# RetNet attention feeding a SwiGLU block: the last 64 tokens of the first batch entry are taken out of the opening and done later, some of q arrives in longer runs, and twelve products are halved

## The chip, the cores and the metric

The kernel runs on one core of a Trainium2 chip. The metric is the device time of one execution in microseconds (us). The engines named below are PE (TensorE: matrix products, with its weight loads listed as PEld), DVE (VectorE), ACT (ScalarE), POOL (GpSimd) and SP (SyncE, which here only issues DMAs). ACT issues DMAs as well.

## The reference

The inputs q, k, v have the shape (8, 8, 576, 64): batch, heads, tokens, head width. The weights are 512 x 1536 (gate and value) and 1536 x 512 (out), all 8 bytes per number in memory.

```python
scores = scale * np.matmul(q, k.transpose(0, 1, 3, 2))
gamma = 1.0 - 2.0 ** (-5.0 - np.arange(H, dtype=np.float32))
Dmat = np.where(rel >= 0, gamma[:, None, None] ** rel[None, :, :], 0.0)   # rel = token i - token j
attn_out = np.matmul(scores * Dmat[None], v)                              # (B, H, S, D)
x = np.ascontiguousarray(attn_out.transpose(0, 2, 1, 3)).reshape(B * S, H * D)   # 4608 x 512
g = x @ w_gate
silu = g * (1.0 / (1.0 + np.exp(-g)))
out = silu * (x @ w_val) @ w_out
```

Because of the causal decay, attention can be done in chunks of 64 tokens: each chunk needs its own 64 x 64 score block and one 64 x 64 state that sums up all chunks before it. 576 tokens are nine chunks, and 576 = 4 x 128 + 64.

## The kernel before, in words

**Attention** works on pairs of heads. There are 8 batch entries of 4 pairs, so pairs 0 to 31; `HP` is 4. `load(i)` (L271) issues the DMAs of pair i. `tick(t)` (L678) is one step of a pipeline three pairs deep: it brings pair t into the right layout (`transposes`), computes scores and states of pair t-1 (`scores`, `new_states`, and the DVE work in `masked`), and finishes pair t-2 (`own_values`, `earlier_values`, then `to_x`, which scales the result by the decay of each row and writes it into x, the transposed input of the second block).

**The first batch entry** (pairs 0 to 3, ticks 0 to 5 with `hi == HP`) is done in an opening in which nothing else can run. There, q and k are transposed by PE through PSUM banks (L471) and copied out by DVE or ACT (L472). The ninth chunk has its own small transposes (L476) and copies (L479), its own scores (L566), mask (L589), values (L554) and a last output (L651). q arrives unscaled, and `to_x` multiplies on DVE (L627, L640).

**The second block** takes x in tiles of columns. The first tile has 512 tokens (`up0`, L767, then `down0`); its weights arrive as 8-byte numbers and are turned into 4-byte ones by two ACT passes (`split`, L404 and L405) and two DVE instructions (`rounding`, L418 and L419). `up0(f, chunks)` multiplies weight block f of gate and value with x, 512 columns at a time. Two `up0` blocks start in the opening. The rest, f = 2 to 11, stand in a list called `plan` (from L1109), with the ticks of the second batch entry between them: tick 4 after f = 2, tick 5 after f = 3, tick 6 after f = 5. From L1163 on, tiles of 1024 tokens use a fast multiplication scheme written out in tables (`up_step` L1003, `down_step` L1050), with the remaining ticks among them.

**What sets the order.** L1085 fixes the order of every engine's instructions, SP's too, to that of the program text: each engine works through its list in order, and an instruction that waits holds up all that follow on the same engine. DMAs issued by SP and by ACT share eight completion semaphores, handed out in turn, so that a DMA waits for the landing of the eighth DMA before it in the order in which the program was laid out, whichever of the two engines issued that one. The list of SP around the change is: the loads of pairs 0 to 3 and small tables, eight weight pieces and more (L385), `load(4)` (`load(HP)`, L1091, emitted in tick 3), one gate weight block (L385), `load(5)` (`load(HP + 1)`, L1097), then `load(6)` (from `next_load`, L1122). ACT issues the later weight loads between its passes (L385 for up weights, L387 for w_out).

The index i of `load(i)`, the argument of `up0` and the argument of `tick` are used below as in the code.

Of the kernel before, what the change touches and what calls it, by code (L numbers as in the profile page):

```python
# [22 lines left out]
def tables(gamma, scale, L):  # L23
# [12 lines left out]
    pieces = scale * np.stack(half, axis=2).reshape(2 * L, -1)  # L36
    parts = [twice((g[:, None] ** -at).T), twice((g[:, None] ** (L - at)).T),
             both(g[:, None] ** L), both(g[:, None] ** (2 * L)), pieces, both(scale * g[:, None] ** at),
# [116 lines left out]
def kernel(  # L155
# [32 lines left out]
    nc = tc.nc  # L188
# [65 lines left out]
    io = const.tile([P, 1024], F32, name="io")  # L254

# [8 lines left out]
    def whole(i):  # L264

        return i < needed(2) - 2
# [4 lines left out]
    def load(i):  # L271
# [6 lines left out]
        if i < HP:  # L278
            qk = late[0] if late else ld.tile([P, 2, S // SQ, SQ], F32, tag="qk", name="qk").rearrange("p n j d -> p (n j d)")[:, 0 : NC * D]
            queues = (nc.sync, nc.scalar if i < 2 else nc.sync)  # L280
            for dst, src in ((qk, q), (kn, k)):
                dst = dst.rearrange("p (g d) -> p g d", d=D)
                for n, at in enumerate((slice(0, NFULL + 1), slice(NFULL + 1, NC))):
                    queues[n].dma_start(out=dst[:, n::2], in_=tokens(src, b, p)[:, at])
            queues[i % 2].dma_start(out=t.rearrange("p (g d) -> p g d", d=D), in_=tokens(v, b, p))
# [21 lines left out]
    def chunk(i, hl, c, paired=False):  # L307

        if whole(i):
            g, r = divmod(NC * hl + c, 2)  # L310
            g = 2 * g % NC if paired else g
            return half[r], slice(g * D, (g + 1) * D)
        if c + 1 == NC:
            return half[hl], slice(CW, CW + D)
        return half[c % 2], slice((2 * (c // 2) + hl) * D, (2 * (c // 2) + hl + 1) * D)

    def column(i, hl, c):

        return ts((c - hl) % NC if i < HP else c, L)
# [6 lines left out]
    NCOL = 2 * H + 4 * HP  # L326
# [8 lines left out]
    piece = tab[:, NCOL - 2 * HP : NCOL]  # L335
# [12 lines left out]
    decay(slice(0, H), slice(0, H), half[0])  # L348
    decay(odd_heads, even_heads, half[1])
    decay(even_heads, odd_heads, half[1])  # L350
    nc.gpsimd.tensor_copy(out=last_near, in_=near[:, even_heads])
# [71 lines left out]
    for f in range(2):  # L423
        for m in range(2):
# [8 lines left out]
    spare = rest[:, dn_at + 2560 : sum_at]  # L433
    other = (spare[:, 0:CW].rearrange("p (h c i) -> p h c i", h=2, i=L), spare[:, CW : CW + L],
             spare[:, 640 : 640 + NC * D].rearrange("p (c d) -> p c d", d=D))
    early = [spare[:, 640 + S * (1 + i) : 640 + S * (2 + i)] for i in range(HP)]
# [6 lines left out]
    def last_scores(i):  # L443
        return bankE[:, 0:L] if i < HP else sr
# [14 lines left out]
    def transposes(i):  # L459
# [7 lines left out]
        if i < HP:  # L467

            for t, src, bank in ((kT, kn, bankB), (qT, qk, bankA)) if i else ((qT, qk, bankA), (kT, kn, bankB)):
                for c in range(NFULL):  # L470
                    nc.tensor.transpose(bank[:, ts(c, P)], src[:, ts(c, P)], ident)  # L471
                copy(t[:, 0:CW], bank)  # L472
            tails = ((kT, kn), (qT, qk))
            for n, (_, src) in enumerate(tails):
                for hl in range(2):
                    nc.tensor.matmul(bankC[half[hl], ts(n, L)], src[half[hl], CW : CW + D], ident[half[hl], half[hl]],  # L476
                                     start=True, stop=True, skip_group_check=True)
            for n, (t, _) in enumerate(tails):
                copy(t[:, CW:S], bankC[:, ts(n, L)])  # L479
# [13 lines left out]
        def keys():  # L493
            blocks = kn.rearrange("p (g d) -> p g d", d=D)
            if i < HP:
                parts = [(0, every, blocks[:, 0 : NC - 1 : 2]), (1, every, blocks[:, 1:NC:2]), (1, half[1], blocks[half[1], NC - 1])]
            elif whole(i):
# [38 lines left out]
    def new_states(i):  # L536
        s = st[i]
        for c in range(NFULL):
            for r in range(2):
                for hl in range(2):  # L540
                    rows, at = chunk(i, hl, 2 * c + r)
                    nc.tensor.matmul(z[half[hl], r, c], s["kn"][chunk(i, hl, 2 * c + r, i < HP)], s["v"][rows, at],  # L542
                                     start=True, stop=True, skip_group_check=True)

    def earlier_values(i):
# [6 lines left out]
        for hl in range(2):  # L552
# [3 lines left out]
        for c in (1, 3, 4, 6, 5, 7, 2, 8) if whole(i) else range(1, NC):  # L556
            for hl in range(2):
                nc.tensor.matmul(xr[half[hl]] if c + 1 == NC else value(i, hl, c), state[half[hl], c, :],  # L558
                                 s["qT"][half[hl], column(i, hl, c)], start=False, stop=True, skip_group_check=True)
# [656 lines left out]
```

## Time and profile before

| | |
|---|---|
| time, three runs | 1041.9 us median, 1040.08 to 1045.64 |
| the profiled execution: its own time / its span | 1040.84 us / 1039.1 us |
| PE busy | 1025.6 us, 99% of the span |
| PE busy before 26.39 us, when `up0` begins | 18.91 of 26.39 us |
| PE busy from 44.00 to 73.00 us | 29.0 of 29.0 us |
| DVE, ACT, POOL busy | 642.3, 297.4, 400.5 us |
| mean busy share of the 16 DMA engines, first 26.39 us | 1.00 |
| the same, 44.00 to 52.30 / 52.30 to 59.60 us | 0.95 / 0.84 |
| PE clock granted | 0.999 |

Lines such as L772 are those of the kernel before. In a row of the timeline the first number is the start (us from the start of the span), the second the time to the end of the last instruction of the row, then follow engine, line, operation, what is written and read, how many, and in brackets the time that the engine idled before and what ended it. One product of 4-byte numbers is two matmul records[...]. SPq and ACTq rows are DMA issues, not transfers.

### The profile page before, as it was taken

Reading aid. Unit: us, or ns where it says so; the run is one execution under the profiler, and the core shown is the slowest. Engines: PE = TensorE matmul, PEld = TensorE weight load, DVE = VectorE, ACT = ScalarE, POOL = GpSimd, SP = SyncE. Lnnn points to the kernel's source line nnn. Section 1 sums busy time; section 2 is a strip of 40 time slices with the busy share of each in tenths; the row PEclk is TensorE's granted clock in tenths of the full one; section 3 lists DMA queues with packets and bytes.
Section 4 is the critical chain, followed back from the end, with each engine's and each line's share of the span. In section 5 each row is a group of like instructions: output and inputs, shape, how many; then the busy total and the mean of one; then the engine's idle time right before and its main releaser. Section 6 shows DMA issues by size and latency. Waiting matters only on the chain.

```text
span 1039.1 us, 21528 instructions
## 1 busy us (share of the span) xinstructions
PE 1025.6 (99%) x8448; PEld 843.2 (81%) x8448; DVE 642.3 (62%) x1091; ACT 297.4 (29%) x646; POOL 400.5 (39%) x347
## 2 busy tenths in 40 slices
PE   7999999999999999999999999999999999999998
PEld 6444555888888888888888888888888888888887
DVE  5588868776768767546458785435466644344644
ACT  4475433243544222222322103223211022231110
POOL 2002376766565036522133058212240583222505
PEclk9999999999999999999999999999999999999999
DMA  9999877776679887674676686545554465555653
GB/s 244 251 283 276 190 208 270 195 212 191 195 190 256 213 249 217 186 196 134 186 229 173 176 202 216 152 138 153 158 172 150 143 195 154 152 153 162 180 162 100
DMA packets 310380, 199.10 MB, mean 192 GB/s; under 512 B 220168, under 2 KB 254984, under 8 KB 310280
## 3 DMA queue, kind: packets, MB, share of 16 engines
q1 hardware_dynamic: 279000, 161.51, 57.3%
q10 hardware_dynamic: 31280, 36.22, 10.4%
q8 instruction: 67, 1.10, 0.4%
q14 instruction: 33, 0.27, 0.1%
HBM read 157.56 MB, written 40.11 MB: 190 GB/s over the span
## 4 chain that ended last, share of the span: by engine, by line
PE 78%; DVE 2%; issue 1%; ACT 0%; DVEq 0%
PE bankC L1003 13%; PE bankE L1003 13%; PE bankB L1003 13%; PE bankA L1003 13%; PE bankB L1050 6%; PE bankC L1050 6%; PE bankA L1050 6%; PE bankE L1050 6%; PE outer L531 1%; PE inner L572 1%; PE outer L558 1%; PE inner L542 1%; DVE rest L806 1%; DVE arena L806 0%; DVE rest L940 0%
## 5 line engine op out<-in xcount | busy, mean ns | idle before, releaser
L940 POOL TENSOR_TENSOR rest<-rest 128x512 f32<-128x512 f32 x65 | 91.6, 1414 | 299.1 <-DVE rest L940 279.8
L1024 ACT ACTIVATE io<-rest 128x256 f32<-128x256 f32 x180 | 74.8, 416 | 303.5 <-DVE rest L940 260.8
L1003 PE MATMUL bankC<-rest,arena 128*128 128x256 f32 x544 | 129.1, 380 | 0.0
L1003 PE MATMUL bankA<-rest,arena 128*128 128x256 f32 x544 | 128.7, 379 | 0.0
L806 POOL TENSOR_TENSOR arena<-arena 128x512 f32<-128x512 f32 (+1 forms) x72 | 111.5, 1561 | 36.1 <-DMA up<-arena 23.9
L1003 PE MATMUL bankE<-rest,arena 128*128 128x256 f32 x512 | 121.4, 380 | 0.9 <-DVE rest L940 0.9
L1003 PE MATMUL bankB<-rest,arena 128*128 128x256 f32 x512 | 121.2, 379 | 0.0
L1031 POOL TENSOR_TENSOR arena<-rest,io 128x256 f32<-128x256 f32 x72 | 51.9, 726 | 167.8 <-ACT io L1024 167.8
L1003 PEld LDWEIGHTS bankA<-rest,arena 128*128 128x128 f32 x544 | 103.2, 190 | 14.5 <-issue 0.5
L1003 PEld LDWEIGHTS bankC<-rest,arena 128*128 128x128 f32 x544 | 102.9, 190 | 14.6 <-POOL arena L806 0.3
L1003 PEld LDWEIGHTS bankE<-rest,arena 128*128 128x128 f32 x512 | 96.9, 190 | 14.6 <-DVE rest L940 1.4
L1003 PEld LDWEIGHTS bankB<-rest,arena 128*128 128x128 f32 x512 | 97.1, 190 | 13.3
L806 POOL TENSOR_TENSOR rest<-rest 128x256 f32<-128x256 f32 (+1 forms) x66 | 67.4, 1042 | 95.9 <-DMA qk<-in_k_dram 60.1
L940 DVE TENSOR_TENSOR rest<-bankB,rest 128x512 f32<-128x512 f32 x72 | 48.9, 687 | 67.4 <-PE bankB L1003 51.5
L940 DVE TENSOR_TENSOR rest<-bankC,rest 128x512 f32<-128x512 f32 x72 | 48.9, 687 | 65.8 <-PE bankC L1003 47.1
L940 DVE TENSOR_TENSOR rest<-bankA,rest 128x512 f32<-128x512 f32 x72 | 48.9, 687 | 61.5 <-PE bankA L1003 44.1
L940 DVE TENSOR_TENSOR rest<-bankE,rest 128x512 f32<-128x512 f32 x71 | 48.2, 687 | 60.0 <-PE bankE L1003 46.7
L1027 DVE SCALAR_TENSOR_TENSOR arena<-rest,io 128x256 f32<-128x256 f32 x84 | 58.5, 698 | 11.1 <-ACT io L1024 11.0
L1050 PE MATMUL bankB<-arena 128*128 128x256 f32 x252 | 58.3, 381 | 0.3 <-DVE arena L806 0.3
L1050 PE MATMUL bankA<-arena 128*128 128x256 f32 x252 | 58.0, 380 | 0.2 <-DVE arena L806 0.2
L1050 PE MATMUL bankC<-arena 128*128 128x256 f32 x252 | 58.1, 380 | 0.0
L1050 PE MATMUL bankE<-arena 128*128 128x256 f32 x252 | 57.9, 379 | 0.0
(192 smaller groups left out, 1617.0 us busy)
## 6 DMA issues: line engine op xcount, KB each, us to landing
arena<-up SPq DMA_DIRECT2D x234, 256.0 KB, 2.6
arena<-dn SPq DMA_DIRECT2D x104, 384.0 KB, 3.8
up<-arena ACTq DMA_DIRECT2D x78, 256.0 KB, 4.1
dn<-rest SPq DMA_DIRECT2D x78, 128.0 KB, 1.9
out_dram<-rest SPq DMA_DIRECT2D x31, 256.0 KB, 4.1
qk<-in_q_dram SPq DMA_DIRECT2D x108, 72.0 KB, 2.3
qk<-in_k_dram SPq DMA_DIRECT2D x108, 72.0 KB, 3.3
rest<-in_moe_w_out_dram ACTq DMA_DIRECT2D x6, 1024.0 KB, 5.1
```

The lines of the kernel that those rows point to most:

```text
L531: m = nc.tensor.matmul(value(i, hl, c), s["v"][rows, at], ret[rows, c % 2 if whole(i) else hl, c // 2], start=start, stop=start, skip_grou ...
L542: nc.tensor.matmul(z[half[hl], r, c], s["kn"][chunk(i, hl, 2 * c + r, i < HP)], s["v"][rows, at], start=True, stop=True, skip_group_check= ...
L558: nc.tensor.matmul(xr[half[hl]] if c + 1 == NC else value(i, hl, c), state[half[hl], c, :], s["qT"][half[hl], column(i, hl, c)], start=Fal ...
L572: nc.tensor.matmul(sc[chunk(i, hl, 2 * c + r)[0], r if whole(i) else hl, c], kT[half[hl], at], qT[half[hl], at], start=True, stop=True, sk ...
L806: eng.tensor_tensor(out=dst, in0=srcs[0], in1=srcs[1], op=ALU.add if op[0] == "add" else ALU.subtract)
L940: eng.tensor_tensor(out=at(op[1]), in0=at(op[2]), in1=at(op[3]), op=ALU.add if op[0] == "add" else ALU.subtract)
L1003: m = nc.tensor.matmul(b[:, gv * TB : (gv + 1) * TB], w[:, gv, ts(c, P)], rhs[:, c, :], start=(opens and gv == 0 and c == 0), stop=(c == 1 ...
L1024: nc.scalar.activation(out=s, in_=src[:, 0:TB], func=AF.Silu, scale=-1.0 if negative else 1.0)
L1027: return lambda: nc.vector.scalar_tensor_tensor(out=dst, in0=src[:, TB : 2 * TB], scalar=-1.0, in1=s, op0=ALU.mult, op1=ALU.mult)
L1031: nc.gpsimd.tensor_tensor(out=dst, in0=src[:, TB : 2 * TB], in1=s, op=ALU.mult)
L1050: nc.tensor.matmul(b[:, m * TB : (m + 1) * TB], lhs[:, qd, ts(m, P)], w[:, qd], start=(opens and qd == 0 and m == 0), stop=(qd == NQ - 1), ...
```

## The change

- **Ninth chunk.** In the opening, pairs 0 to 3 are loaded, transposed and multiplied only for tokens 0 to 511 (`CW`). The work of L476, L479, L554, L566, L589 and L651 is gone from there. The last state of each pair is written to a new place, `end_states`.
- **Where it goes.** `end_loads` issues 20 DMAs on SP after `load(5)`: 16 that bring q and k of the 64 tokens of all eight heads, 16 KB each in runs of 128 bytes, and four for v. `end_transposes` (two DVE block transposes of 128 x 256) stands in `plan` ahead of tick 5; `end_scores` (8 products) follows the scores of pair 4 on PE inside tick 5; `end_masks` (two DVE multiplies) closes the DVE pieces of tick 5; `end_own`, `end_earlier` (8 products each) and `end_to_x` (three DVE multiplies) are in tick 6.
- **q of pairs 1 to 3** is loaded with four consecutive tokens per partition, in runs of 1 KB rather than 256 bytes, into `early[i]`; `scale_run` multiplies it on POOL by the scale and the row's decay while regrouping it, and `transposes` undoes the interleaving while copying out of PSUM. `to_x` of these pairs is then a plain copy on ACT instead of a multiply on DVE.
- **Loads of pairs 0 to 3** go by head: six DMAs of 128 KB per pair instead of five of 288, 160 or 128 KB.
- **Order in tick 3.** `split(0)` moves ahead of pair 1's values, and the transposes of pair 3 move behind `to_x` of pair 1.
- **Decay tables.** The opening builds them with two POOL instructions instead of three; the swapped halves and `last_near` are made after `load(5)`. The table of `run` adds 32 columns to the first small DMA.
- **Twelve products.** `up0(2)` (gate and value) and the gate half of `up0(3)` do each of their four products as two of 256 columns.

```diff
-        return i < needed(2) - 2
+        return HP <= i < needed(2) - 2
+
+    def scaled(i):
+
+        return 0 < i < HP
...
-            for dst, src in ((qk, q), (kn, k)):
-                dst = dst.rearrange("p (g d) -> p g d", d=D)
-                for n, at in enumerate((slice(0, NFULL + 1), slice(NFULL + 1, NC))):
-                    queues[n].dma_start(out=dst[:, n::2], in_=tokens(src, b, p)[:, at])
-            queues[i % 2].dma_start(out=t.rearrange("p (g d) -> p g d", d=D), in_=tokens(v, b, p))
+            for h, queue in zip(heads, queues):
+                if scaled(i):
+                    queue.dma_start(out=early[i][:, ts(h % 2, CW // 2)], in_=q[b, h, 0:CW].rearrange("(p c) d -> p (c d)", c=NFULL))
+                else:
+                    queue.dma_start(out=blocks(qk)[:, h % 2], in_=q[b, h, 0:CW].rearrange("(c p) d -> p c d", p=P))
+            for h, queue in zip(heads, queues):
+                queue.dma_start(out=blocks(kn)[:, h % 2], in_=k[b, h, 0:CW].rearrange("(c p) d -> p c d", p=P))
+            for h in heads:
+                queues[i % 2].dma_start(out=blocks(t)[:, h % 2], in_=v[b, h, 0:CW].rearrange("(c p) d -> p c d", p=P))
...
+                if scaled(i):
+                    nc.scalar.copy(out=dst(lo, end)[to].rearrange("p (c r i) -> p c r i", r=2, i=L)[:, :, r], in_=xo[src, :, r])
...
+    def end_loads():
+        for n, src in enumerate((q, k)):
+            for a in range(P // SQ):
+                for j in range(2):
+                    nc.sync.dma_start(
+                        out=end_raw[a * SQ : (a + 1) * SQ, n].rearrange("t (n j d) -> t n j d", n=HP, d=SQ)[:, :, j],
+                        in_=src[0, a // 2 : H : 2, CW + j * SQ : CW + (j + 1) * SQ, (a % 2) * SQ : (a % 2 + 1) * SQ].rearrange("n t d -> t n d"))
+        for hl in range(2):
+            for x in range(2):
+                nc.sync.dma_start(out=end_v[half[hl ^ x], 2 * x : 2 * x + 2],
+                                  in_=v[0, 4 * x + hl : 4 * x + 4 : 2, CW:S].rearrange("n t d -> t n d"))
+    def end_transposes():
+        for n, to in enumerate((end_q, end_k)):
+            nc.vector.transpose(out=to.rearrange("p n i -> p (n i)"), in_=end_raw[:, n])
+    def end_scores():
+        for n, x, hl in ends:
+            nc.tensor.matmul(end_at[x][half[hl ^ x], n], end_k[half[hl], 2 * x + n], end_q[half[hl], 2 * x + n],
+                             start=True, stop=True, skip_group_check=True)
+    def scale_run(i):
+        if scaled(i):
...
+            nc.gpsimd.tensor_tensor(out=dst, in0=src, in1=table, op=ALU.mult)
...
+            scale_run(t + 1)
             if lo < t < hi:
                 new_pair()
+            if t + 1 == HP:
+                split(0)
             if lo <= t - 2 < hi:
                 own_values(t - 2)
-            for f in transposes(t) if lo <= t < hi else ():
+            for f in transposes(t) if lo <= t < hi and t + 1 < HP else ():
                 f()
-            if t + 1 == HP:
-                split(0)
...
+            for f in transposes(t) if t + 1 == HP else ():
+                f()
...
             scores(t - 1, t - 2 < lo)
+            if t == HP + 1:
+                end_scores()
...
+                if f == 2 or f == 3 and gv == 0:
+                    for m in range(2):
+                        nc.tensor.matmul(bank[:, ts(m, TB)], w, xs[0][:, c, ts(m, TB)],
+                                         start=(c == 0 and m == 0), stop=(c == HP - 1), skip_group_check=True)
+                    continue
...
     load(HP + 1)
+    for to, heads in ((even_heads, odd_heads), (odd_heads, even_heads)):
+        decay(heads, to, half[1])
+    nc.gpsimd.tensor_copy(out=last_near, in_=near[:, even_heads])
+    end_loads()
...
+            if tick_at[f] == HP + 1:
+                plan.append(end_transposes)
             plan.append(lambda t=tick_at[f]: tick(t, HP, FIRST))
```

## The prediction

> **What bounds the kernel now.** I read the page first. PE is busy almost throughout; the only slice below nine tenths is the first.
>
> ```profile
> PE 1025.6 (99%) x8448; PEld 843.2 (81%) x8448; DVE 642.3 (62%) x1091; ACT 297.4 (29%) x646; POOL 400.5 (39%) x347
> ...
> PE   7999999999999999999999999999999999999998
> ```
>
> So a change pays only by shortening the opening, and whatever stops PE later is lost in full: no engine can catch up for it. The timeline of PE shows where the opening ends and what stops it last: the values of pair 2 wait for `to_x` of pair 1 on DVE, and `up0` starts at 26.39.
>
> ```profile
> 24.88 1.01 PE L531 MATMUL outer<-ret,v 64*64 64x64 f32 x32 [1.52 <-DVE rest L627]
> ...
> 26.39 0.70 PE L772 MATMUL bankA<-rest,arena 128*128 128x512 f32 x1
> ```
>
> Next, the place where the moved work goes, tick 5. PE computes pair 4's states (L542) and scores (L566, L572) at 57.8 and goes straight on with `up0(4)` at 59.01; these rows show no idle time:
>
> ```profile
> 57.81 0.69 PE L542 MATMUL inner<-v,kn 64*64 64x64 f32 x32
> ...
> 58.44 0.64 PE L572 MATMUL inner<-qT,kT 64*64 64x64 f32 x30
> 59.01 3.70 PE L772 MATMUL bankA<-rest,arena 128*128 128x512 f32 x8
> ```
>
> Last, SP's timeline and its waits, because the moved chunk must first be loaded and its 20 DMAs stand behind `load(5)`:
>
> ```profile
> 49.01 2.77 SPq L293 DMA_DIRECT2D qk<-in_k_dram  x4
> 51.87 0.45 SPq L298 DMA_DIRECT2D kn<-in_k_dram  x1
> 59.57 0.39 SPq L298 DMA_DIRECT2D v<-in_v_dram  x1
> 60.05 4.10 SPq L293 DMA_DIRECT2D qk<-in_q_dram  x4
> ```
>
> ```profile
> SPq L298 <- DMA rest<-in_moe_w_out_dram: 9.0, 2, 7.2
> ```
>
> v of pair 5 is issued at 59.57, 7.2 us after the DMA ahead of it. It waits for a w_out block that ACT issued at 53.16: that DMA is the eighth before it, and the two share a completion semaphore. SP passes the end of `load(5)` at 59.96, after PE has gone through the place where `end_scores` will stand.
>
> ACT's timeline says why w_out is late: its `split` waits 5.71 us for the gate block that SP issued at 43.10.
>
> ```profile
> 50.74 0.67 ACT L404 ACTIVATE rest<-rest 128x512 f32<-128x512 f32 x1 [5.71 <-DMA rest<-in_moe_w_gate_dram]
> ...
> 53.16 0.39 ACTq L387 DMA_DIRECT2D rest<-in_moe_w_out_dram  x1
> ...
> 57.36 0.37 ACTq L385 DMA_DIRECT2D rest<-in_moe_w_val_dram  x1
> ```
>
> **What the Trainium skill says.** "DMA: Bandwidth & Descriptors", section "Anatomy of one DMA — SWDGE (gpsimd) path", says that DMA engines never wait on semaphores; the issuing sequencer waits before it dispatches. The trace agrees: for those 7.2 us SP issues nothing. The same section puts a DMA's fixed cost at about 2 us; here four k pieces landed a median 2.2 us after issue (48 to 52 us) and 5.3 us under a weight load (64 to 68 us). "Why small descriptors are slow (HBM only)" on that page charges a fixed overhead per packet; from 5 to 13 us, all in 256-byte runs, the trace has 281 GB/s, against 369 to 430 in slices where 2 KB runs dominate. "TensorE: Matmul & The Clock Gate", section "Architectural detail", lets PE pull only weight loads ahead of running products; the trace of before cannot show whether `up0(4)` could overtake a waiting `end_scores`, and I take it that it cannot.
>
> **The change, part by part.**
>
> *The opening.* Per pair the tails (L476, two small copies L479) go: in tick 3 they take PE from 21.72 to 22.27, and elsewhere the scores start about 0.4 us after the big q copy could have allowed them (tick 1: that copy ends at 12.60, scores start at 13.03). Over ticks 0 to 2 about 1.0 us stays on the path. The reordering of tick 3 lets PE do pair 3's transposes (1.1 us) after pair 1's values, beside `to_x`, and takes most of the 1.52 us wait away; `to_x` moves to ACT (three copies, 0.37 each by `even`'s L583), behind `split(0)` (two passes, 0.67 each). Estimate: `up0` starts 2.6 us earlier, between 1.5 and 3.5.
>
> *DMA.* 4 pairs x 3 tensors x 128 runs = 1536 runs of 256 bytes go (0.39 MB; at 281 GB/s 1.4 us). q of three pairs, 0.79 MB, in 1 KB runs at perhaps 370 instead of 281 GB/s saves 0.7. Together SP and the weights come 2.1 us earlier. `scale_run` has not been traced; POOL's 128x512 multiply (L940) takes 1.41 us, three of them 4.2 us on an engine busy 7.29 us of the first 26.39. It stands ahead of the keys of pairs 2 and 3 on POOL, so a late q would delay those by at most its lateness. I take zero; 1 us at worst, spent in the opening.
>
> *Twelve products.* 48 half-width records in place of 24. Full ones come every 0.43 us; halves in the later tiles (L1003) every 0.215 (eight in 1.72 us), with a weight load of 190 ns under each. Cost 0; at worst 48 x 0.025 = 1.2 us.
>
> *The moved work.* 24 products = 48 records on PE. The 32 records of L558 take 0.57 us there (73.95 to 74.52), so 0.9 us. DVE gains two transposes (128x576 takes 0.77, so 0.35 each), two masks and three scalings, about 2 us in all, which lie under `up0`.
>
> *The wait.* `end_scores` needs both `end_transposes`, and these need the 16th DMA of `end_loads`. Before time minus 2.1: w_out lands at 57.4 (59.5 before), v of pair 5 goes then, E1 to E3 to 59.2. E4 stands where the DMA eight before it is the next weight block (issued by ACT at 57.36 before; SP got past it at 62.58), so 60.4. Twelve more issues at about 0.45 us (rows of 0.39 to 0.50 where SP is free): E16 at 65.8. Landing 2.2 to 5.3, I take 3: 68.8. DVE: +0.7 = 69.5. In before's time PE left this point at 59.01. **Delay 10.5 us, plus 0.9 for the moved products: 11.4.** The opening's 2.6 us do not count: PE only reaches the wait earlier (about 56.4) and stands there for some 13 us. Behind `end_scores` on PE are `up0(4)` and everything after; behind `end_transposes` on DVE the masks of pair 4 and the roundings, which hold up `split` on ACT. After the release, DVE stands to PE about as before (60.30 against 59.01), so I add nothing for it; `load(6)` follows the 20 issues and keeps its distance to tick 6.
>
> Sum on the profiled execution: 1040.84 + 11.4 = 1052.2. This execution lies 1.1 us below the median. The positions of the shared semaphores are the least known term and the errors I can name (0.35 us per issue, a quick landing) shorten the wait, so I put the likeliest at 1051.
>
> **Rivals.**
>
> *A. SP is not held behind w_out.* If the layout gives other eighth neighbours, v goes at 49.8 + 0.5, 16 issues take 7.2, landing 2.2, transposes 0.7: release at 60.4, 1.4 us after 59.01; with 0.9, +2.3 us: 1043 (1041 to 1046). For: the number of DMAs ahead changes. Against: all move by the same four places, and w_out and the value block are still among the eight in front of some E; whichever waits for w_out cannot go before 57.
>
> *B. The loads arrive before PE needs them* (the other side). Then the opening's 2.6 us stay, less 0.9: 1039. It decides at a landing of E16 by 55.7 (PE at 56.4, less 0.7), so E1 would have to be issued by 55.7 - 2.2 - 15 x 0.45 = 46.7; SP is at the last of `load(5)`'s k at 49.8 even unhindered. PE would show no gap at tick 5.
>
> *C. A longer hold.* The gate block that ACT issued at 61.93 (landing at about 67.5 before, when ACT's L404 at 67.87 waits for its queue) is the eighth before one of E9 to E16, and the stalled DVE makes later weights late too: another 3 to 6 us, 1055 to 1058. For: its issue lies just after those of `load(5)`.
>
> **How the numbers follow.** Main case 0.66 (1047 to 1055); A 0.18; B 0.07; C 0.07; something in the opening worth over 5 us 0.02. About 0.5% (5 us) is what a measurement of this kernel tells from no change. Slower takes the main case, C and a sliver of A: 0.75; same is A and B: 0.23; faster 0.02, since even B gives only 0.2%. The range 1042 to 1056 leaves out B, most of C and the edges; the main case's own is 1047 to 1055.
>
> **What would show it.** Right: one idle stretch of PE of 8 to 15 us ahead of the first `end_scores` product, released by DVE's transpose, itself released by a DMA into `rest` from q or k; `up0` at about 24; no idle time at the halved products; SP's 20 issues starting only after a wait for a weight DMA. Wrong: the issues start before 50 us, PE passes tick 5 without a gap, or products behind `end_scores` run ahead of it.

## The result, and the profile after

The changed kernel takes 1058.3 us (median of four runs, 1056.81 to 1058.58) beside 1041.5 us for the kernel before (1040.08 to 1045.64). The ratio is 1.0147, with an interval of 1.0125 to 1.017: 15 us slower by the ratio, 17 by the two medians. The forecast of 1051.0 had the direction, but the time lies above its range (1042 to 1056).

One execution of each kernel was profiled; that of the changed one took 1058.58 us with a span of 1056.9. Its page (busy time by engine, then tenths of 40 slices and the granted TensorE clock in the same slices):

```profile
PE 1024.3 (97%) x8440; PEld 845.0 (80%) x8440; DVE 640.9 (61%) x1078; ACT 300.2 (28%) x648; POOL 401.6 (38%) x349
...
PE   6949999999999999999999999999999999999998
...
PEclk9979999999999999999999999999999999999999
```

PE's busy time is 1.3 us less than before, while the span is 17.8 us longer: PE does not work more, it stands. The third slice (53 to 79 us) shows it with a 4, and a clock of seven tenths. A record below is one matmul instruction as the profile lists it. PE's timeline there (start, duration, engine, line, operation; in brackets the idle time ahead and what ended it):

```profile
57.09 0.67 PE L574 MATMUL inner<-qT,kT 64*64 64x64 f32 x30
72.44 0.71 PE L704 MATMUL outer<-rest 64*64 64x64 f32 x16 [14.67 <-DVE rest L698]
73.07 4.99 PE L852 MATMUL bankA<-rest,arena 128*128 128x512 f32 x8
```

PE finishes the scores of pair 4 at 57.76 and then waits 14.67 us for the second DVE transpose of the moved chunk. `up0(4)` starts at 73.07 instead of 59.01, 14.06 us later. Its first eight records take 4.99 us; before they took 3.70.

SP's timeline and its waits from 40 to 75 us show where the transposes' data was:

```profile
39.15 4.50 SPq L392 DMA_DIRECT2D rest<-in_moe_w_gate_dram  x1
...
59.54 0.38 SPq L311 DMA_DIRECT2D v<-in_v_dram  x1
60.02 5.24 SPq L688 DMA_DIRECT2D rest<-in_q_dram  x8
65.37 5.01 SPq L688 DMA_DIRECT2D rest<-in_k_dram  x8
```

```profile
SPq L311 <- DMA rest<-in_moe_w_out_dram: 7.4, 1, 7.4
SPq L392 <- ACT rest L412: 4.0, 1, 4.0
SPq L688 <- DMA rest<-in_moe_w_val_dram: 1.5, 1, 1.5
SPq L688 <- DMA rest<-in_q_dram: 1.1, 1, 1.1
```

v of pair 5 is issued at 59.54, no earlier than before (59.57), after the same wait for w_out. The fourth of the 20 loads waits for the value block, and the eleventh waits 1.1 us for the fourth. (The trace also holds the number of each DMA's completion semaphore: w_out and v have 102, the value block, the fourth and the eleventh load 106.) The line with 4.0 us is taken up below, where the prediction is compared. The sixteenth load, the last one of k, goes at 69.95, and on DVE the transposes follow their loads:

```profile
68.45 0.45 DVE L698 STREAM_TRANSPOSE rest<-rest 128x256 f32<-128x256 f32 x1 [8.59 <-DMA rest<-in_k_dram]
71.93 0.45 DVE L698 STREAM_TRANSPOSE rest<-rest 128x256 f32<-128x256 f32 x1 [3.04 <-DMA rest<-in_k_dram]
```

The rest of the trace adds little. `up0` starts at 23.63 instead of 26.39, and in this execution the loads gain nothing from it: v and w_out come when they came before. (Traces of one opening differ: three with that of before start `up0` at 25.12, 26.39 and 27.61, the fourteen with the new one between 23.63 and 25.46. The means lie 1.9 us apart.) In tick 6 the moved products add 0.78 us. In the second tile PE waits twice more, where the kernel before has one wait of 0.95 us at 190.80:

```profile
204.24 1.96 PE L1082 MATMUL bankA<-rest,arena 128*128 128x256 f32 x8 [1.68 <-DVE rest L1019]
...
210.43 1.99 PE L1082 MATMUL bankC<-rest,arena 128*128 128x256 f32 x8 [0.51 <-POOL arena L1053]
```

PE starts the second tile 16.17 us later than before (190.32 against 174.15), and from the 201st record of that tile on it is 17.7 us late, to the end. The following comparison of starts (us, one profiled execution each) serves all the experiments:

| kernel | first down product | second tile | its 201st record | last product |
|---|---|---|---|---|
| before | 123.77 | 174.15 | 218.88 | 1034.91 |
| after | 139.94 | 190.32 | 236.62 | 1052.67 |
| chunk not moved | 121.62 | 175.66 | 223.18 | 1038.84 |
| scores one tick later | 125.97 | 177.87 | 223.53 | 1040.29 |
| loads first | 128.87 | 181.22 | 228.22 | 1045.06 |
| v of pair 5 behind the loads | 139.91 | 190.29 | 234.06 | 1050.28 |
| loads on GpSimd's queue | 130.26 | 180.64 | 225.21 | 1041.97 |
| the same, transposes ahead of `up0(3)`'s product | 128.93 | 179.78 | 225.25 | 1043.25 |
| the same, ahead of `up0(2)`'s product | 124.13 | 176.47 | 222.00 | 1038.78 |
| before, 13.8 us of products | 137.00 | 187.50 | 230.96 | 1047.58 |
| after, stretch filled | 137.31 | 188.93 | 234.13 | 1049.82 |
| after, products undivided | 144.65 | 196.29 | 240.58 | 1056.36 |
| before, v of pair 5 cut in five | 124.65 | 175.03 | 219.10 | 1035.35 |

### The profile page after: what moved, and what is told of

Same layout as the page of the kernel before. It is cut to its first block, busy times and chain, and to the rows that moved or that the text cites. A ratio compares the mean times of both kernels' runs of the same rounds, so it can differ in the third digit from the quotient of the medians.

```text
span 1056.9 us, 21545 instructions
## 1 busy us (share of the span) xinstructions
PE 1024.3 (97%) x8440; PEld 845.0 (80%) x8440; DVE 640.9 (61%) x1078; ACT 300.2 (28%) x648; POOL 401.6 (38%) x349
## 3 DMA queue, kind: packets, MB, share of 16 engines
q10 hardware_dynamic: 30784, 36.18, 10.3%
## 4 chain that ended last, share of the span: by engine, by line
PE 67%; DVE 3%; SPq 1%; ACT 1%; issue 0%; DMA 0%; ACTq 0%; POOL 0%; DVEq 0%
PE bankE L1082 11%; PE bankC L1082 11%; PE bankB L1082 10%; PE bankA L1082 10%; PE bankB L1129 6%; PE bankA L1129 5%; PE bankC L1129 5%; PE bankE L1129 5%; PE outer L533 1%; PE outer L560 1%; PE inner L574 1%; PE inner L544 1%; SPq L306 1%; DVE rest L885 1%; DVE rest L1019 0%; DVE arena L1106 0%
## 5 line engine op out<-in xcount | busy, mean ns | idle before, releaser
L1019 DVE TENSOR_TENSOR rest<-bankC,rest 128x512 f32<-128x512 f32 x72 | 48.9, 688 | 65.8 <-PE bankC L1082 47.1
L1019 DVE TENSOR_TENSOR rest<-bankE,rest 128x512 f32<-128x512 f32 x71 | 48.3, 688 | 59.5 <-PE bankE L1082 46.6
```

The lines of the kernel that those rows point to most:

```text
L1019: eng.tensor_tensor(out=at(op[1]), in0=at(op[2]), in1=at(op[3]), op=ALU.add if op[0] == "add" else ALU.subtract)
```

## The experiments

**Is it SP's order and the shared semaphores?** Four kernels change where the loads stand, or when they are needed.

Leave the moved chunk out (the last 64 tokens of the first batch entry are missing from the output; their columns of x are set to zero):

```diff
-    end_loads()
+    nc.gpsimd.memset(xs[1][:, :, 0:L], 0.0)
```

and without the calls of `end_transposes`, `end_scores`, `end_masks`, `end_own`, `end_earlier`, `end_to_x`.

> The changed kernel without the moved chunk: its 20 loads, transposes, scores, masks, values and scalings are left out, so the 64 tokens of the first batch entry are missing from the output (their columns of x are zero). Theory (the loss is PE's wait for the moved loads): no idle stretch at tick 5, up0 at about 23.6 us, a time of 1041.5 less 2.8 for the opening and less up to 1 us at the second tile, 1037.5 to 1039.5 us. Rival (the opening's other edits, q through POOL, the loads by head or the halved products, cost time further on): over 1045 us.

Measured 1045.71 us, ratio 1.0031 (1.0015 to 1.0047). The stretch in tick 5 is gone: `up0(4)` starts at 56.86. But the time is not 1039: it lies where the rival had it, over 1045. The first down product is 2.15 us earlier than before, and the last product is 3.9 us later. What takes it back is treated below.

Need the scores one tick later:

```diff
-            if t == HP + 1:
+            if t == HP + 2:
                 end_scores()
```

with `end_transposes` and `end_masks` in that tick as well, and `end_own`, `end_earlier`, `end_to_x` in the next.

> The loads stay where they are; the transposes, scores and masks of the moved chunk go from tick 5 to tick 6, its values and scalings from tick 6 to tick 7. Theory: the last k load lands at about 72 us, PE reaches tick 6 at about 71 us, so at most 1 us of idle time is left there and the time is 1039 to 1042 us. Rival (20 small DMAs on SP cost as much wherever the products stand, since the loads of pairs 6 and 7 come 13 us later behind them): PE waits at tick 6 or 7 for these pairs instead, 1048 us or more.

Measured 1050.04 us, ratio 1.0083 (1.0056 to 1.0111). The stretch shrinks from 14.67 to 1.96 us, at 74.53, so the wait is one for data that comes at a fixed time. The whole time was missed and lies where the rival had it, though the wait that is left in tick 6 is for the transposes of the moved chunk, not for pairs 6 and 7: the profiled run, the quickest of its four (1046.2), already shows 1.29 us of waiting at 166.84.

Put the 20 loads ahead of those of pair 5:

```diff
+    end_loads()
     load(HP + 1)
     ...
-    end_loads()
```

> The 20 loads stand ahead of the load of pair 5 instead of behind it. In this layout the w_out block is the eighth DMA before the 16th load. Theory (position in SP's queue and the shared semaphore make the wait): the first 15 go between 44 and 52 us, the 16th when w_out has landed, 57 to 60 us; PE idles at tick 5 until 60 to 62 us, for 2 to 5 us; the time is 1042 to 1047 us. If only the number of DMAs mattered: the idle stretch stays near 14 us and moves to pair 5, 1055 us or more. If neither the semaphore nor w_out mattered: no idle stretch, 1039 to 1041 us.

Measured 1049.99 us, ratio 1.0072 (1.0053 to 1.0092); PE waits 3.62 us at 61.13. Same loads, same bytes, eleven microseconds less of a wait. The sixteenth load went at 57.27, when w_out had landed, as expected. The whole time was again missed, by later waits (1.44 us at 147.45, 2.36 at 195.83).

Put v of pair 5 behind the 20 loads, so that the first of them, not v, is the eighth DMA behind w_out:

```diff
-            for dst, src in ((kn, k), (t, v)):
+            for dst, src in ((kn, k), (t, v))[: 1 if i == HP + 1 else 2]:
```

and v of pair 5 after `end_loads()`.

> The v load of pair 5 stands behind the 20 loads instead of ahead of them; now the first of the 20 is the eighth DMA behind w_out. Theory (whatever stands eighth is held): the first load is issued at 59 to 60 us, as the v load was, and PE idles 13 to 15 us at tick 5. Rival (the v load waited for its own buffer): the first load is issued at about 52 us and the idle stretch shrinks to 7 or 8 us.

Measured 1056.2 us, in one execution. SP's timeline, then PE's:

```profile
50.92 0.44 SPq L311 DMA_DIRECT2D kn<-in_k_dram  x1
59.59 4.38 SPq L688 DMA_DIRECT2D rest<-in_q_dram  x8
```

```profile
71.43 0.71 PE L704 MATMUL outer<-rest 64*64 64x64 f32 x16 [14.39 <-DVE rest L698]
```

Now a load of q stands for w_out, up to the same 59.6 us. What waits is the place, whichever transfer holds it (here w_out and this load of q have semaphore 102). With the run before this, that shows the prediction's mechanism.

**The loads on another queue.** GpSimd's queue instead of SyncE's:

```diff
-                    nc.sync.dma_start(
+                    nc.gpsimd.dma_start(
                         out=end_raw...
```

(and the same for `end_v`).

> The 20 loads of the moved chunk go through GpSimd's queue instead of SyncE's; nothing else differs from after. Theory (the 14.7 us stretch comes from SyncE's issues standing behind w_out and the gate block through shared semaphores): the loads no longer stand there, they are issued from about 40 us on, and the idle stretch of PE at end_scores falls from 14.7 to between 0 and 5 us. For the whole time the theory says no more than what the run with the scores one tick later showed: 1044 to 1050, since the later passages take some back. Rival (the 20 loads are slow in themselves, by their small runs): the stretch stays above 10 us and the time at 1055 to 1060.

Measured 1047.09 us, ratio 1.005 (1.0035 to 1.0065), beside 1058.3 (1.0147) for the change as it is, and as expected. The 20 loads are issued from 31.88 to 46.7 us and have all landed at 51.83, so small runs were not the trouble. PE still waits 2.83 us at 61.24, for a transpose that DVE did at 60.43, behind its product of `up0(3)`.

Move the transposes ahead of that product too:

```diff
+        if f == 3:
+            plan.append(end_transposes)
         plan.append(lambda f=f: up0(f, range(HP)))
...
-            if tick_at[f] == HP + 1:
-                plan.append(end_transposes)
```

> The 20 loads on GpSimd's queue as in the earlier run, and the two DVE transposes ahead of the product of up0(3) instead of behind it. Theory (what was left there, 2.83 us, was DVE's order, not the loads): PE passes tick 5 with no idle time over 0.3 us, at about 58 us. Time: down0 then starts at about 127.5, some 3.5 us behind before; with the passage up to 200 us taking 0 to 3 us, 1044 to 1048. Rival (POOL's issues or the loads themselves cost it): the idle time stays above 2 us.

Measured 1046.01 us, ratio 1.0037 (1.0022 to 1.0052). Its time was met, its reason was not: 2.08 us of waiting are left, as the rival had it. DVE's timeline shows that the rival's cause is not it either: the data has long landed, but the roundings of the weights (L425, L426) stand ahead of the transposes until 59.2.

```profile
58.57 0.69 DVE L426 CUSTOM_DVE_ANT_0 arena<-arena,rest 128x1024 uint16<-128x1024 uint16 x1
59.18 0.76 DVE L698 STREAM_TRANSPOSE rest<-rest 128x256 f32<-128x256 f32 x2
```

So `if f == 2:` in place of `if f == 3:`, which puts them where DVE stood idle:

> The 20 loads on GpSimd's queue, and the two DVE transposes ahead of the product of up0(2), where DVE stood idle until about 55 us, instead of ahead of that of up0(3), where the roundings kept them until 59.2. Theory (the rest of the wait was DVE's order, and the slow products come from the wait): PE passes tick 5 at about 58 us without idle time over 0.6 us and the first eight records of up0(4) take 3.7 us. That is 4.8 us less up to the first down product, 124. What arrives at the end: if PE's time is passed on, 1041 to 1042.5; if the passage from 125 to 200 us takes it as it did without the chunk, 1044 to 1047. Rival for the wait (it is the data): 2 us stay.

Measured 1043.05 us, ratio 0.9999 (0.9985 to 1.0014). The second rival has fallen: DVE transposes at 53.95, and PE goes from the scores of pair 4 into `end_scores` and `up0(4)` without a stop, at full pace:

```profile
58.22 0.45 PE L704 MATMUL outer<-rest 64*64 64x64 f32 x15
58.59 3.70 PE L852 MATMUL bankA<-rest,arena 128*128 128x512 f32 x8
```

With everything that the change adds, and the wait taken away by moving the loads and the transposes, the kernel takes what it took before, to within 1.5 us: the wait and its slow products are the loss. No gain is left either. `up0` starts 2.2 us earlier than before, `up0(4)` only 0.4 earlier (58.59 against 59.01), since PE waits 0.74 us for keys on ACT and 0.54 for `kT` earlier in tick 5, and moved products come on top.

**Halving the twelve products.** Undo it:

```diff
-                if f == 2 or f == 3 and gv == 0:
+                if False:
```

> After with the twelve products of the first tile undivided, as before. Prediction: halving costs nothing, so 1058.3, within 1.5 us, and PE reaches up0(4) at the same time (73.1, within 0.3). Rival (two records of 256 columns cost more than one of 512, by up to 0.1 us each): 1.2 us or more less, 1057 or below, and seen in the distance from up0 to tick 5.

Measured 1060.05 us, ratio 1.0167 (1.0147 to 1.0187), where the change has 1.0125 to 1.017. It is, if anything, slower undivided, so halving costs nothing that can be told. PE reaches `up0(4)` at 72.07, a microsecond earlier than expected: the stretch ahead is 14.26 us in this run. Its profiled execution is the slowest of its four (1062.3) and has a second stop that no other trace shows and that the profile puts down to nothing, with slow products behind it:

```profile
93.75 0.62 PE L574 MATMUL inner<-qT,kT 64*64 64x64 f32 x25 [2.33 <-issue]
```

So this trace can't price the halving further on.

**The slow products behind the stretch.** Fill the stretch with products whose sums are not used:

```diff
             if t == HP + 1:
+                for m in range(30):
+                    nc.tensor.matmul(banks[0], w_up[:, 0, 0, 0, 0, 0:P], xs[0][:, 0, :], start=True, stop=True)
                 end_scores()
```

> After with 30 further 512-column products (12.9 us at 0.43) into a bank that up0(4) then overwrites, ahead of end_scores; their sums are not used. PE is busy for nearly all of the time in which it stood. Theory (the slow products after the stretch come from PE having stood): the first eight of up0(4) take 3.7 us again instead of 4.99, the stretch left is about 1.8 us, and the time is about 1.3 us less than after, 1057. Rival (the products are slow because DVE, ACT and the loads run beside them): they take 4.9 again and the time stays 1058.

Measured 1066.83 us. The size of the edit was wrong: a 512-column product of this kernel is two records of 0.43 us, not one, so the 30 products take 25.9 us, to 82.6, and nothing is left to wait for. The number in dispute can still be read: the first eight records of `up0(4)` take 3.70 us. With 16 products (13.8 us):

> After with 16 further 512-column products (13.8 us) ahead of end_scores, into a bank that up0(4) then overwrites; their sums are not used. They fill the stretch in which PE stood and leave about 1 us of it. Theory (the slow products after the stretch come from PE having stood): the first eight records of up0(4) take 3.7 us, not 4.99, end_scores starts at 72.4 as in after, and the time is 1.3 us less or more, 1054 to 1057. Rival (the spell comes from what DVE and ACT do there): 4.9 again, time 1058.

Measured 1055.09 us, ratio 1.0126 (1.011 to 1.0142). That is where the theory had it, but the interval overlaps that of the change (1.0125 to 1.017); PE's timeline decides:

```profile
56.14 14.00 PE L788 MATMUL bankA<-rest,arena 128*128 128x512 f32 x32
71.37 0.46 PE L704 MATMUL outer<-rest 64*64 64x64 f32 x16 [1.23 <-DVE rest L698]
71.77 3.70 PE L854 MATMUL bankA<-rest,arena 128*128 128x512 f32 x8
```

`end_scores` starts a microsecond earlier than in the change itself; it is through in 0.40 us instead of 0.63, and the first eight records in 3.70 instead of 4.99. The windows view (busy time of each engine, then the granted clock, DMA share and GB/s) from 72 to 76 us, first of the change, then of this run:

```profile
72.00:76.00 4.00, 3.56 (x20) 1.88 (x21) 3.54 (x10) 0.00 (x0) 0.00 (x0) 0.54 0.39 72
```

```profile
72.00:76.00 4.00, 4.00 (x10) 1.77 (x10) 3.86 (x12) 0.00 (x0) 0.00 (x0) 1.00 0.50 87
```

DVE is as busy in both, ACT and POOL idle in both, and the DMA engines are busier in the run with the quick products (0.50 against 0.39), so the rival has nothing left; the clock is 0.54 against 1.00. The products are slow because PE had stood. "TensorE: Matmul & The Clock Gate" of the Trainium skill has this in "Part 1: The HAM clock gate": after an idle window of about 3.4 us the PE clock falls to half, and it takes a busy window of about that length to release it. The half agrees (records of 0.85 us where 0.43 is usual). Less idle time than the page's window was enough here: the run with the transposes ahead of `up0(3)`'s product waited 2.08 us, between short 64x64 products, and its `up0(4)` starts like this:

```profile
59.99 0.71 PE L704 MATMUL outer<-rest 64*64 64x64 f32 x16 [2.08 <-DVE rest L698]
60.63 6.46 PE L852 MATMUL bankA<-rest,arena 128*128 128x512 f32 x8
```

That is 2.8 us lost behind a wait of 2.08; behind the 14.67 us of the change it was 1.3. The loss does not grow with the wait: over the seven runs with a wait of 1.96 to 14.67 us there it was 1.3 to 2.8 us, least in the change itself. The short wait costs more than twice its length. But not every stop of two microseconds does this. PE stops as long in the second tile of the run with the loads first, and at 165.44 in the last GpSimd run, and the records behind keep their usual pace, with a granted clock of 1.00:

```profile
195.83 1.97 PE L1082 MATMUL bankA<-rest,arena 128*128 128x256 f32 x8 [2.36 <-DVE rest L1019]
```

```profile
165.44 0.69 PE L560 MATMUL outer<-qT,state 64*64 64x64 f32 x32 [1.73 <-DVE state L609]
166.06 1.12 PE L863 MATMUL bankA<-rest,arena 128*128 128x512 f32 x2
```

What decides it for a short stop is not shown.

**Is a late PE made up for later?** The kernel before, with the same 16 products in tick 5:

```diff
             scores(t - 1, t - 2 < lo)
+            if t == HP + 1:
+                for m in range(16):
+                    nc.tensor.matmul(banks[0], w_up[:, 0, 0, 0, 0, 0:P], xs[0][:, 0, :], start=True, stop=True)
```

> The kernel before, with 16 further products of 512 columns (two records of 0.43 us each, 13.8 us in all) in tick 5 behind the scores of pair 4; their sums are not used. It delays PE there by about what the change does, without the change, the wait or an idle PE. Theory (a delay of PE in tick 5 is lost in full): 1042 + 13.8 = 1055.8, between 1054 and 1058. Rival (the passages behind, paced by other engines, swallow part of a late PE): 1052 or less.

Measured 1054.87 us, ratio 1.0125 (1.0108 to 1.0142), or 11.3 to 14.8 us more. 13.8 is inside: PE's lost time is lost, less perhaps one microsecond (from the second tile to its 201st record it takes 43.46 us instead of 44.73). This kernel, with none of the change, is as slow as the change with its stretch filled (1055.09).

**What took the opening's gain back?** In the run without the moved chunk PE's timeline shows a stop, and slow products behind it:

```profile
162.98 0.70 PE L560 MATMUL outer<-qT,state 64*64 64x64 f32 x32 [1.79 <-DVE state L609]
163.62 2.07 PE L852 MATMUL bankA<-rest,arena 128*128 128x512 f32 x2
165.48 1.76 PE L852 MATMUL bankB<-rest,arena 128*128 128x512 f32 x2
167.08 1.02 PE L852 MATMUL bankC<-rest,arena 128*128 128x512 f32 x2
```

1.79 us of waiting and 1.8 us of slow products turn a lead of 2.15 us at the first down product into a lag of 1.5 at the second tile; two waits (1.62 us at 189.54, 1.77 at 196.99), in place of one of 0.95, add 2.8 more. The DVE chain behind the stop waits 3.23 us for a store of `dn<-rest` at 160.19, which before is 1.04 us at 159.29. In that passage POOL has little room. Its busy time is the fifth pair in the windows from 140 to 170 us, before, then without the moved chunk:

```profile
140.00:170.00 30.00, 29.91 (x396) 15.95 (x396) 23.23 (x40) 8.08 (x26) 28.86 (x34) 1.00 0.65 214
```

```profile
140.00:170.00 30.00, 28.12 (x277) 13.97 (x270) 21.33 (x37) 8.09 (x26) 28.56 (x35) 0.94 0.61 201
```

POOL's weight sums ahead of it wait for stores too. Before, one store releases POOL at 133.76 and another at 137.26; without the chunk POOL waits until 137.51 and comes to the same second sum at 138.34, although PE is 2 us earlier. So a PE that comes early finds its operands no earlier. Is early arrival all of it? Delay PE again, by products in tick 5, first 6, then 3 of them, with the chunk left out:

```diff
             if t == HP + 1:
-                end_scores()
+                for m in range(6):
+                    nc.tensor.matmul(banks[0], w_up[:, 0, 0, 0, 0, 0:P], xs[0][:, 0, :], start=True, stop=True)
```

> The run without the moved chunk (the last 64 tokens of the first batch entry are left out, so its output lacks them), with six further 512-column products (2.6 us at 0.43) in tick 5, whose sums are not used: PE is then as late from tick 5 on as in the kernel before or 0.4 us later. Theory (the stage from 125 to 200 us is paced by SyncE's stores and the weight sums on POOL and DVE, and PE that comes early only stands there): the added 2.6 us are not added to the end; the waits at 163, 190 and 197 us shrink and the time is at or below that run's 1045.7, between 1041 and 1046. Rival (what that run lost after 125 us comes from the edits themselves, not from PE's being early): 2.6 us more than it, 1048 or 1049.

> The run without the moved chunk (the last 64 tokens of the first batch entry are left out) with three further 512-column products (2.6 us) in tick 5, whose sums are not used. PE is then about 0.5 us later than in the kernel before from tick 5 on. Theory (the opening's gain is lost because PE only arrives early at a passage that others pace): no dearer than without them, 1044 to 1046.5. Rival (PE's time is lost one for one there too): 1048.3.

For the first the size was off by two, as above: its products take 5.2 us, so neither of its two outcomes can be held to its numbers. Measured 1047.69 us with six (ratio 1.0058, 1.0037 to 1.008), 1046.50 with three (1.0038, 1.0024 to 1.0052), beside 1.0031 with none. Of 5.2 us added the ratios show 2.8, of 2.6 they show 0.7; the intervals are too wide to exclude a full loss. The traces decide more: the waits do not vanish, as the theory wanted. With three products PE reaches the first down product 1.7 us later than before, and yet waits 1.22 us at 166.30, 2.11 at 191.69 and 0.99 at 199.88. Early arrival alone is not the cause.

The other suspect was that four more DMAs shift who shares a completion semaphore with whom. Cut v of pair 5 into five loads, in the run without the chunk and in the kernel before:

```diff
-                    queue.dma_start(out=dst.rearrange(...), in_=tokens(src, b, p))
+                    for lo, up in ((0, 32), (32, 64), (64, 96), (96, 112), (112, P)) if i == HP + 1 and src is v else ((0, P),):
+                        queue.dma_start(out=dst.rearrange(...)[lo:up], in_=tokens(src, b, p)[lo:up])
```

> The run without the moved chunk (the last 64 tokens of the first batch entry are left out), with the one load of v of pair 5 cut into five by rows: the same bytes, four more DMAs, so that from there on every DMA has the same neighbours on the eight shared semaphores as in the kernel before. Theory (which DMAs share a semaphore decides the passage from 125 to 200 us): the waits at 163, 190 and 197 us go back to those of before, one of about 1 us at 190; time 1038.5 to 1041.5. Rival (it is PE's early arrival, or the different work of the opening): 1045.7 as without the cut, within 1.5.

> The kernel before with the same cut of the load of v of pair 5: four more DMAs, so that from there on the neighbours on the semaphores are those of the run without the moved chunk. Theory (neighbours): slower than before by 3 to 6 us, 1045 to 1048, with waits of PE near 190 and 200 us of 1.5 us or more. Rival: 1042 within 1.5.

Measured 1046.52 us (ratio 1.0023, 1.0008 to 1.0039) and 1042.19 (ratio 0.9989, 0.9977 to 1.0002). Both go the rival's way: the neighbours do not decide this passage. (The edit did what it should: of the 739 DMAs of SyncE behind it, 725 have the semaphore that they have in the other kernel, in both pairs.) What makes POOL's sums and DVE's states there one to two microseconds later with the changed opening stays open; that POOL paces the passage is read from the traces, not tried. What is shown is that the opening's gain does not reach the end, and where it stops. One thing does not fit: the last GpSimd run has the same opening and more work, and its ratio is lower (0.9999 against 1.0031), although its one trace is late behind this passage as well (222.00 against 218.88). So the 3 us are a figure of the run without the chunk, not the price of the new opening in every kernel.

## Why the prediction was wrong

**Right.** The bound and the place: one idle stretch ahead of the first `end_scores` product, released by DVE's transpose, itself released by a load of k. The cause: SP held by position behind w_out (shown by the runs on order and on the other queue). PE does not run ahead of a waiting `end_scores`. The twelve products: nothing. The opening does not count in the sum. The loss is passed on (12.3 us by the medians for 13.8 added in the kernel before). The opening's 2.76 us at `up0`, where 2.6 was taken, are partly luck: over all traces the means differ by 1.9.

Two steps failed: the row of loads was priced too low, and the clock was left out.

**Wrong in size: E1 to E16.** E1 to E16 are the 16 loads of q and k in their order. Five traces have the same loads in the same places up to tick 5:

| trace | SP's gate block | w_out landed | v | E4 | E11 | E16 | `end_scores` |
|---|---|---|---|---|---|---|---|
| forecast | | 57.4 | 57.4 | 60.4 | | 65.8 | 69.5 |
| after | 39.15 to 43.65 | 59.48 | 59.54 | 63.05 | 67.40 | 69.95 | 72.44 |
| products undivided | 39.19 to 40.89 | 57.65 | 57.71 | 61.50 | 66.38 | 68.93 | 71.43 |
| stretch filled (16) | 37.98 to 39.64 | 56.70 | 56.77 | 61.04 | 66.30 | 68.83 | 71.37 |
| stretch filled (30) | 38.84 to 40.59 | 57.53 | 57.59 | 62.29 | 67.78 | 70.31 | not waiting |
| scores one tick later | 38.18 to 39.95 | 57.10 | 57.16 | 59.93 | 64.97 | 67.50 | in tick 6 |

From v to E16 it took 10.3 to 12.7 us in all five, where 8.4 stood. "Twelve more issues at about 0.45 us" left out that these loads hold each other up: E11 stood for 1.1 to 1.9 us until E4 had landed, which by position is the eighth DMA before it. The wait of E4 for the value block was foreseen, and v to E4 took 2.8 to 4.7 us where 3.0 stood. From E16 to the release it took 2.5 us where 3.7 stood, which gives 1.2 back. In the three traces that show the release it is 1.9 to 2.9 us late.

**"Together SP and the weights come 2.1 us earlier", as carried to w_out,** failed in the profiled execution, where w_out landed at 59.48 (before: 59.50), and held in the other four. In the profiled one SP reached the gate block at 39.15 and was through with it 4.5 us later. The view above puts 4.0 us of this down to an ACT pass at 42.39 (`split`, L412, reading `x_odd`). That can't be the reason. With the products undivided, the same instructions, the block was issued ahead of that pass:

```profile
39.19 1.71 SPq L392 DMA_DIRECT2D rest<-in_moe_w_gate_dram  x1
42.57 0.69 ACT L412 ACTIVATE rest<-x_odd 128x512 int32<-128x512 uint32 x1
```

What held the issue for 4.5 us is not shown. Nor does the late issue explain w_out: with v behind the loads the gate block was issued by 40.99 and w_out at 51.89 instead of 52.66, and w_out still landed at 59.52. What makes w_out land near 57 in some executions and near 59.5 in others stays open. The release differs by one microsecond only between the two kinds.

**Not foreseen: the clock.** The forecast priced the products behind the wait as if PE had never stopped: "After the release ... I add nothing". The slow spell costs 1.3 us in `up0(4)` and 0.2 in `end_scores`; in the two other runs with a wait of 14 us it was 2.1 and 2.7 in `up0(4)`.

**Mis-sized: the moved products**, 0.63 + 0.78 = 1.41 us for 0.9, half of the difference being that spell. **And the passage into the second tile** costs 1.6 us more than before in this pair of executions (46.30 us instead of 44.73), which the sum had as nothing. With v behind the loads, a PE just as late needs 43.77 us for it, so this term may be chance.

The sum by measured terms of the two profiled executions: 72.44 - 59.01 = 13.4 for the wait, 1.4 for the products, 1.3 for the clock, 1.6 for the passage, together 17.7; the span grew by 17.8. The forecast's 11.4 lacks 2.9 + 0.5 + 1.3 + 1.6 = 6.3 of it. Of the 2.9, 2.1 lie ahead of v in this execution. The 1.2 us that it took off for a quick landing made it a little worse.

One reading was loose, with nothing hanging on it: from 5 to 13 us, 7948 of the 8076 packets were short ones, not all.

**The rivals.** A fell: SP is held. B fell twice over. The loads are late, and with them in time the opening's gain still does not reach the end: 1043.05 where B had 1039. C came near the right time (1055 to 1058) for the wrong reason. Its place was right: the gate block that ACT issued, at 61.38 here, and E12 have one semaphore, 107. But the block had all but landed: E12 went at most 0.4 us late (at 68.17, with E11 issued by 67.71).

## What to carry to other kernels

Price a row of loads by what stands eight places before each of them, the row itself included, and not by the issue times alone: here the sum of issues gave 8.4 us and the chip took 10.3 to 12.7. Price a stall of the matrix engine with the slow spell that can follow it, 1.3 to 2.8 us behind the waits of ticks 5 and 6, even for a stop of 2 us. And semaphores shared by position are a dependency that no line of the program shows: 20 small loads on another queue, and two transposes ahead of the roundings, took the whole loss away, to within 1.5 us. A last point is on reading: a line of a wait view names what ended last by its own inference. Where the same instruction went ahead of the named one in another trace, the name is wrong.

## What was not expected of the hardware

A stop of 1.79 us at 162.98, between short products, was followed by record pairs of 2.07 and 1.76 us instead of 1.02. One of 1.73 us at the same place in another run was not followed by any, nor was one of 2.36 us in the second tile. GpSimd's queue issued 16 KB loads at one per 0.55 us and landed them 3.3 to 6.2 us later; it waited twice, 1.38 and 2.22 us, for loads of its own, and not for the transfers that held SyncE's.
